# Two attentions on one core: A's maxima and sums in three halving steps, and additions moved from GpSimd to VectorE

## The chip, the cores and the metric

The kernel runs on one core of one Trainium2 chip. The metric is the device time of one execution in microseconds (us): the kernel before has a median of 1677.7 us over three runs (1677.5 to 1679.12).

The engines go by the profile's names: PE is TensorE (matmuls; PEld its weight loads), DVE is VectorE, ACT is ScalarE, POOL is GpSimd, and SP is SyncE, which issues nearly all DMA transfers. Each engine takes its instructions strictly in the order in which the program emits them, and an instruction that waits holds up all behind it on the same engine.

## The reference

Two attention layers over a sequence of 2048 positions, 576 features, 32 heads of 18 features, each with its own input, weights and output projection; their outputs stand side by side.

```python
# A: each position attends to itself and the 7 positions 2, 4, ... 14 before it
logits = jnp.einsum("bhsd,bhswd->bhsw", q, kg) * scale      # kg: 8 gathered keys per position
logits = jnp.where(mask[None, None, :, :], logits, -1e9)
attn = _softmax(logits, axis=-1)
o = jnp.einsum("bhsw,bhswd->bhsd", attn, vg)
# B: full attention, all 2048 keys
p = _softmax(jnp.einsum("bhqd,bhkd->bhqk", q, k) * scale, axis=-1)
o = jnp.einsum("bhqk,bhkd->bhqd", p, v)
# each: o (2048 x 576) @ wo
```

## The kernel before, in words

A first phase projects both inputs; the main loop (line 1099) is B's attention, and A's work is strewn into it.

**The main loop** has 512 steps: 8 groups of 4 heads, 4 blocks of 512 queries, 16 tiles of 128 keys. In one step TensorE makes four score tiles (`score`, L227, into four banks called "scores"), ScalarE takes their exponentials (L233), and TensorE weighs the values with those of the step before (`weigh`, L700, eight matmuls into `po`). Beside the scores TensorE forms three, in some steps four, score tiles of a later block (`take`, L162), of which VectorE keeps only the row maxima (`reduce`, L169). These go into a ring of three banks called "else": a fourth maximum's matmul must wait until VectorE has reduced the first.

**The order of the work** is written out by hand. `agenda` holds for each step a list of functions; `due` (L1114) calls them after that step's scores and weighing have been emitted, so what they emit stands on each engine between two steps' work. `plan(start, pieces)` enters functions at offsets from a start, `later(n, f)` at n steps from now. Nothing ties GpSimd's or SP's progress to the steps but the data: a step number gives only the place in the queue. `inside` holds functions that are called between the scores of the next step.

**A's attention** comes in 8 tiles j of 256 positions. `local(j)` makes the plan of a tile, which starts at step 10 + 54 j; offsets below are counted from there, so offset 59 of one tile is offset 5 of the next. The tile's 128 partitions hold 32 heads in 4 pieces of 64 positions. In order of the plan:

- `arrange(n)` (L802), n = 0, 1, 2 for q, k, v: a DRAM-to-DRAM transfer of A's projections into the tile's arrangement (`dpart<-da`, 576 or 702 KB), at offsets -24 to -22; `fetch` (L808) brings q (0), k (1) and v (28) from there into `aq` and `akv`.
- `match(c)` (L821), c = 0 to 8, at offset 5 + 5c // 2: on GpSimd a product of q and the 8 shifted keys for two features (L823) and, from c = 1 on, its addition (L827); the last one, at 25, also makes the 8 logits per position, `lg` (L830).
- `most` (29) and `lower` (30): VectorE reduces the maximum over the 8 into `am` (L837), GpSimd subtracts it (L844). `exponents` (32) on ScalarE. `total` (34): VectorE sums into `as` (L837) and takes its reciprocal (L851). `share` (35): GpSimd multiplies (L854).
- `weighted(c)` (L856), c = 0 to 8, at 36 + 5c // 2: four GpSimd instructions (L860 to L863) into the output `ao`.
- `upper` (58) and `rest` (59): GpSimd rounds the output into `aohi` (L867) and leaves the remainder in `ao` (L872). `put(0)`, `put(1)` (66, 67) store both to DRAM; `get` (74 and 81) brings them back transposed (`at`, `ahl`).
- `finished` leads to `sums_of_a` (L895) within the steps of offsets 79, 81, 86 and 88: the output projection for 128 positions and half the columns, with two maxima among its matmuls. `beside` (L965) returns two partial sums, `one` in a bank of "scores" and `two` in one of "else"; ScalarE copies `one` into `y` (L904), VectorE copies `two` into `part` (L905), GpSimd adds (L906).

GpSimd also serves B. After each 16 steps `finish` normalises a block's output with three instructions (L734 with `rec`, L735, L736) at 17 to 19 steps from the block's end; `halve` splits B's maxima (L107, L108). SP's queue carries, among others, the loads of B's rows for the next groups (`stack_loads`, L138 to L150, twelve transfers of 288 KB at steps 64 (g - 2) + 1 and on), `rec` (L733) and A's transfers.

Of the kernel before, what the change touches and what calls it, by code (L numbers as in the profile page):

```python
# [7 lines left out]
F32 = mybir.dt.float32  # L8
F32R = mybir.dt.float32r
BF16 = mybir.dt.bfloat16  # L10
AF = mybir.ActivationFunctionType
ALU = mybir.AluOpType
# [7 lines left out]
DH = 18  # L20
# [28 lines left out]
def ap(t, *dims):  # L49

    return bass.AP(tensor=t.tensor, offset=t.offset, ap=[list(t.ap[0])] + [list(d) for d in dims])
# [8 lines left out]
def two_attentions(ctx: ExitStack, tc, xa, wa, woa, xb, wb, wob, c_id, c_sel, out):  # L60
# [56 lines left out]
    def plan(start, pieces):  # L117
        for n, f in pieces:
            agenda[start + n].append(f)
# [100 lines left out]
    def score(g, b, kt, h, also, kind="scores"):  # L220

        assert (g, b) in placed
        qs, ks = sets[g % 3]
        p, r = divmod(h, 2)
        ps = bank(kind)
        at = slice(64 * r, 64 * r + 56)
        nc.tensor.matmul(ps, ks[at, p, 128 * kt : 128 * kt + 128], qs[at, b, p], start=True, stop=True)  # L227
        reduce = maximum(1 - r) if also else None

        counted[0] += 1  # L230
        early = counted[0] % 8 < 6
        e = (e_room if early else work).tile([128, 512], F32, name="e", bufs=6 if early else 2)
        nc.scalar.activation(e, ps, AF.Exp, scale=SCALE)  # L233
        if reduce:
            reduce()
        return e
# [560 lines left out]
    def local(j):  # L797

        st = {}
        p0 = AB * j  # L800

        def arrange(n):  # L802
            wide = (HALO if n else 0) + SUB
            load(rows(dparts[j][n][0, 0], (wide, D), (D * wide, 4), (1, wide)),
                 rows(da[D * n, HALO + p0 + SUB - wide :], (HALO + S, D), (SUB, 4), (1, wide)))


        def fetch(nm):  # L808
            halo = 0 if nm == "q" else HALO
            n = DH * (halo + SUB)  # L810
            t = st[nm] = work.tile([128, DH, halo + SUB], F32, name="akv" if halo else "aq", bufs=2 if halo else 1)
            load(ap(t, (1, n)), rows(dparts[j]["qkv".index(nm)][0, 0], (n, 128), (1, n)))

        def window(t, c):

            return ap(t[:, 2 * c, HALO:], (HALO + SUB, 2), (-DIL, W), (1, SUB))

        def wide():
            return work.tile([128, 2, W, SUB], F32, name="pr", bufs=2)

        def match(c):  # L821
            pr = wide()
            nc.gpsimd.tensor_mul(pr, ap(st["q"][:, 2 * c], (SUB, 2), (0, W), (1, SUB)), window(st["k"], c))  # L823
            if c == 0:
                st["pr"] = pr
            else:
                nc.gpsimd.tensor_add(st["pr"], st["pr"], pr)  # L827
            if c == DH // 2 - 1:
                lg = st["lg"] = work.tile([128, W, SUB], F32, name="lg", bufs=1)
                nc.gpsimd.tensor_add(lg, st["pr"][:, 0], st["pr"][:, 1])  # L830
                if j == 0:
                    for w in range(1, W):
                        nc.gpsimd.memset(lg[:32, w, : DIL * w], MASKED)

        def over_window(op, name):
            t = work.tile([128, SUB], F32, name=name, bufs=1)
            nc.vector.tensor_reduce(t, st["lg"].rearrange("p w i -> p i w"), axis=AX.X, op=op)  # L837
            return t

        def most():  # L840
            st["m"] = over_window(ALU.max, "am")

        def lower():
            nc.gpsimd.tensor_sub(st["lg"], st["lg"], ap(st["m"], (0, W), (1, SUB)))  # L844

        def exponents():
            nc.scalar.activation(st["lg"], st["lg"], AF.Exp, scale=SCALE)

        def total():
            s = st["s"] = over_window(ALU.add, "as")  # L850
            nc.vector.reciprocal(s, s)  # L851

        def share():
            nc.gpsimd.tensor_mul(st["lg"], st["lg"], ap(st["s"], (0, W), (1, SUB)))  # L854

        def weighted(c):  # L856
            if c == 0:
                st["o"] = work.tile([128, DH, SUB], F32, name="ao", bufs=1)
            at = wide()
            nc.gpsimd.tensor_mul(at, ap(st["lg"], (0, 2), (SUB, W), (1, SUB)), window(st["v"], c))  # L860
            nc.gpsimd.tensor_add(at[:, :, :4], at[:, :, :4], at[:, :, 4:])  # L861
            nc.gpsimd.tensor_add(at[:, :, :2], at[:, :, :2], at[:, :, 2:4])
            nc.gpsimd.tensor_add(st["o"][:, 2 * c : 2 * c + 2], at[:, :, 0], at[:, :, 1])  # L863

        def upper():
            hi = work.tile([128, DH, SUB], F32R, name="aohi", bufs=1)
            nc.gpsimd.tensor_copy(hi, st["o"])  # L867
            st["parts"] = hi, st["o"].bitcast(F32R)

        def rest():  # L870
            hi, lo = st["parts"]
            nc.gpsimd.tensor_sub(lo, st["o"], hi)  # L872

        def put(i):
            load(rows(dao[j, i, 0, 0], (DH * SUB, 128), (1, DH * SUB)),
                 ap(st["parts"][i].bitcast(F32), (1, DH * SUB)))

        def get(n):
            st["x"] = []
            st["n"] = n  # L880
            last = work.tile([128, 128], F32R, name="ahl", bufs=1)
            for i in range(2):
                t = work.tile([128, 4, 128], F32R, name=f"at{i}", bufs=1)
                for s in range(2):
                    load(t.bitcast(F32)[:, :, SUB * s : SUB * s + SUB],
                         dao[j, i, 2 * n + s, :512].rearrange("(c p) n -> p c n", p=128))
                load(last.bitcast(F32)[64 * i : 64 * i + 64].rearrange("p (s n) -> p s n", s=2),
                     rows(dao[j, i, 2 * n, 512], (SUB, 64), (D * SUB, 2), (1, SUB)))
                st["x"].append([t[:, c] for c in range(4)])
            st["x"].append(last)  # L890

        def finished(h):
            inside.append(lambda: sums_of_a(h))

        def sums_of_a(h):  # L895
            his, los = zip(*wo["a"])
            w = his[:4], los[:4], his[4], los[4]
            cols = slice(288 * h, 288 * h + 288)
            if h == 0:
                st["y"] = ys["a", j, st["n"]] = work.tile([128, D], F32, name="y", bufs=3)  # L900
            one, two = beside("scores", *(halves(r, 0, w, st["x"], cols, slice(0, 128), True) for r in range(2)))
            y = st["y"][:, cols]
            part = work.tile([128, 288], F32, name="part", bufs=2)
            nc.scalar.activation(y, one, AF.Copy)  # L904
            nc.vector.tensor_copy(part, two)  # L905
            nc.gpsimd.tensor_add(y, y, part)  # L906

        plan = {0: lambda: fetch("q"), 1: lambda: fetch("k"), 28: lambda: fetch("v"), 29: most, 30: lower,
                32: exponents, 34: total, 35: share, 58: upper, 59: rest, 66: lambda: put(0), 67: lambda: put(1)}
        for c in range(DH // 2):  # L910
            plan[5 + 5 * c // 2] = lambda c=c: match(c)
            plan[36 + 5 * c // 2] = lambda c=c: weighted(c)
        for n in range(3):
            plan[(-24 if j else -7) + n] = lambda n=n: arrange(n)
        for n in range(2):
            at = 74 + 7 * n
            plan[at] = lambda n=n: get(n)
            plan[at + 4] = lambda: finished(0)
            plan[at + 6] = lambda: finished(1)
            producing.update((A_FROM + GAP * j + at + 5, A_FROM + GAP * j + at + 7))  # L920
            plan[at + 12] = lambda n=n: load(out[p0 + 128 * n : p0 + 128 * n + 128, :D], ys["a", j, n])
        return plan


    olds = defaultdict(list)
# [33 lines left out]


    inside = []

    waiting = []

# [92 lines left out]
    ):  # L1057
        plan(start, [(4 * c, lambda k=k, src=src, ch=ch: load_wo(k, src, *ch)) for c, ch in enumerate(chunks)])
    for j in range(NJ):
        plan(A_FROM + GAP * j, local(j).items())  # L1060
    for g in range(1, NG):
        if g > EARLY:
            plan(STEPS * (g - 2) + 1, [(n, f) for n, f in enumerate(stack_loads(g))])
# [35 lines left out]
    while step < ALL:  # L1099
        n, kt = divmod(step, NT)  # L1100
        g, b = divmod(n, NB)
        places = positions(min(4 if behind() > 0 else 3, total - sum(given)))
        es = []
        for h in range(4):

            if inside and h == (3 if 3 in places else 2):
                inside.pop(0)()
            es.append(score(g, b, kt, h, h in places))
        while waiting:
            waiting.pop(0)()  # L1110
        if ready:
            weigh(*ready.pop(0))
        ready.append((g, b, kt, es))
        due()  # L1114
        if waiting:
            waiting.pop(0)()
        step += 1
# [30 lines left out]
```

## Time and profile before

| | |
|---|---|
| median of three runs | 1677.7 us |
| the profiled execution | 1677.95 us |
| its span, from the first to the last instruction | 1676.2 us |
| first weighing of the main loop | at 425.42 us |
| mean granted TensorE clock | 0.998 of full speed |
| PE, DVE, ACT, POOL busy in the span | 99%, 84%, 73%, 60% |
| between 500 and 700 us: DVE, ACT, POOL busy | 179.92, 186.30, 165.47 of 200 us |

A row of the timeline gives start, duration (us), engine, line, operation, what is written from what, shapes and count; equal instructions that follow each other are merged. In square brackets stands the idle time of the engine ahead of the row and what ended it. A row of groups gives count, then busy time and mean ns of one, then idle time. A row of the windows gives the stretch and its length, then the busy time of PE, PEld, DVE, ACT and POOL with their counts, the granted clock, the share of the DMA engines and GB/s.

### The profile page before, as it was taken

The numbers are of one execution on the slowest core, as the hardware profiler recorded it, in microseconds if no ns is written. First come the engines' busy times: TensorE is split into PE (matmuls) and PEld (weight loads), VectorE is DVE, ScalarE is ACT, GpSimd is POOL, SyncE is SP. The second block draws the span as 40 slices with busy tenths as digits, with TensorE's granted clock in tenths as the row PEclk, the third lists the DMA queues.
The fourth block names the chain that finished last, engine by engine and source line by source line (L and its number), as shares of the span: only waits on it lengthen the run. The fifth ranks groups of instructions, "written<-read, shape, count | busy, mean of one in ns | idle before, by whom it ended". The sixth has DMA issues, their size and how long they took to land.

```text
span 1676.2 us, 33705 instructions
## 1 busy us (share of the span) xinstructions
PE 1664.2 (99%) x12994; PEld 922.9 (55%) x12994; DVE 1410.6 (84%) x2318; ACT 1223.3 (73%) x2420; POOL 998.6 (60%) x842
## 2 busy tenths in 40 slices
PE   9999999999999999999999999999999999999998
PEld 7998888887433444344444344444444344344765
DVE  5199999999889989889889988889888989888433
ACT  6423521211999988988988987998988988988444
POOL 2306732100286996986984996986995997812010
PEclk9999999999999999999999999999999999999999
DMA  8938944421624536165247128227526222134101
GB/s 246 242 108 220 264 141 135 139 90 66 94 82 62 142 99 107 59 155 115 66 107 156 64 84 181 70 63 134 132 64 131 76 76 77 35 98 170 57 30 58
DMA packets 186082, 188.37 MB, mean 112 GB/s; under 512 B 114832, under 2 KB 129936, under 8 KB 184192
## 3 DMA queue, kind: packets, MB, share of 16 engines
q1 hardware_dynamic: 181056, 174.66, 40.1%
q0 software_dynamic: 4032, 10.63, 3.1%
q8 instruction: 102, 1.67, 0.4%
q10 hardware_dynamic: 832, 0.92, 0.2%
q14 instruction: 60, 0.49, 0.1%
HBM read 113.30 MB, written 88.12 MB: 120 GB/s over the span
## 4 chain that ended last, share of the span: by engine, by line
PE 89%; POOL 6%; SPq 2%; DVE 1%; DMA 1%; issue 1%; ACT 0%; POOLq 0%; ACTq 0%; DVEq 0%
PE po L700 27%; PE bank L227 21%; PE bank L320 14%; PE bank L162 14%; PE bank L979 7%; PE bank L257 4%; SPq L146 1%; POOL pr L823 1%; POOL pr L860 1%; POOL pr L827 1%; DVE mx L169 1%; POOL pr L861 1%; DMA rec<-drec 1%; PE bank L958 1%; PE bank L181 0%
## 5 line engine op out<-in xcount | busy, mean ns | idle before, releaser
L169 DVE TENSOR_REDUCE mx<-bank 128x1 f32<-128x512 f32 x2048 | 1294.4, 685 | 154.1 <-PE bank L162 132.0
L233 ACT ACTIVATE e<-bank 128x512 f32<-128x512 f32 x2048 | 1060.4, 610 | 108.6 <-PE bank L227 57.1
L162 PE MATMUL bank<-ks,qs 54*128 54x512 f32 x2048 | 757.6, 424 | 5.0 <-DVE mx L169 2.7
L227 PE MATMUL bank<-qs,ks 56*128 56x512 f32 x2048 | 582.9, 425 | 0.0
L227 PEld LDWEIGHTS bank<-qs,ks 56*128 56x128 f32 x2048 | 327.2, 186 | 430.7 <-ACT e L233 403.1
L700 PE MATMUL po<-e,v 128*19 128x512 f32 x4096 | 541.0, 600 | 0.0
L162 PEld LDWEIGHTS bank<-ks,qs 54*128 54x128 f32 x2048 | 342.8, 185 | 34.2 <-DVE mx L169 16.8
L823 POOL TENSOR_TENSOR pr<-aq,akv 128x1024 f32<-128x1024 f32 x72 | 157.9, 2197 | 24.6 <-PE po L700 22.3
L700 PEld LDWEIGHTS po<-e,v 128*19 128x19 f32 x4096 | 69.8, 97 | 181.7 <-issue 170.7
L860 POOL TENSOR_TENSOR pr<-lg,akv 128x1024 f32<-128x1024 f32 x72 | 158.1, 2195 | 0.3
L827 POOL TENSOR_TENSOR pr<-pr 128x1024 f32<-128x1024 f32 x64 | 152.4, 2382 | 5.0
L651 ACT ACTIVATE ohi<-bank 128x512 f32<-128x512 f32 (+1 forms) x56 | 30.4, 595 | 155.2 <-issue 124.4
L320 PE MATMUL bank<-xlo,ahi 64*128 64x512 f32 (+1 forms) x448 | 121.8, 391 | 0.1
L320 PE MATMUL bank<-xhi,alo 64*128 64x512 f32 (+1 forms) x448 | 118.6, 390 | 0.0
L320 PE MATMUL bank<-xhi,ahi 64*128 64x512 f32 (+1 forms) x448 | 115.2, 392 | 0.0
L906 POOL TENSOR_TENSOR y<-y,part 128x288 f32<-128x288 f32 x32 | 25.6, 799 | 117.8 <-DVE part L905 102.4
L861 POOL TENSOR_TENSOR pr<-pr 128x512 f32<-128x512 f32 x72 | 92.4, 1283 | 5.6
L461 POOL TENSOR_TENSOR olo<-olo,ohi 128x512 fp32r<-128x512 f32 x36 | 46.2, 1298 | 68.3 <-ACT ohi L460 67.1
L368 POOL TENSOR_TENSOR alo<-raw,ahi 128x512 fp32r<-128x512 f32 (+1 forms) x14 | 17.6, 1254 | 115.1 <-ACT ahi L367 90.6
L320 PEld LDWEIGHTS bank<-xlo,ahi 64*128 64x128 f32 (+1 forms) x448 | 68.1, 182 | 9.4 <-POOL xlo L368 0.5
L320 PEld LDWEIGHTS bank<-xhi,alo 64*128 64x128 f32 (+1 forms) x448 | 65.4, 182 | 9.1
L979 PE MATMUL bank<-wohi,at 64*128 64x288 f32 x512 | 68.9, 301 | 0.0
(194 smaller groups left out, 1845.4 us busy)
## 6 DMA issues: line engine op xcount, KB each, us to landing
do<-n SPq DMA_DIRECT2D x28, 512.0 KB
da<-ohi SPq DMA_DIRECT2D x52, 256.0 KB
dpart<-da SPq DMA_DIRECT2D x16, 702.0 KB
akv<-dpart SPq DMA_DIRECT2D x16, 702.0 KB
out<-y SPq DMA_DIRECT2D x32, 288.0 KB
qs<-dqk SPq DMA_DIRECT2D x30, 288.0 KB
ks<-dqk SPq DMA_DIRECT2D x30, 288.0 KB
at<-dao SPq DMA_DIRECT2D x64, 128.0 KB
```

Of the source, the lines that this page charges most:

```text
L162: nc.tensor.matmul(ps, qs[at, b, p, 128 * t : 128 * t + 128], ks[at, p, 512 * k : 512 * k + 512], start=True, stop=True)
L169: nc.vector.tensor_reduce(mx[:, r, p, t, k : k + 1], ps, axis=AX.X, op=ALU.max)
L227: nc.tensor.matmul(ps, ks[at, p, 128 * kt : 128 * kt + 128], qs[at, b, p], start=True, stop=True)
L233: nc.scalar.activation(e, ps, AF.Exp, scale=SCALE)
L257: nc.tensor.matmul(ps, a, b, start=c == i == 0, stop=c == 4 and i == 1)
L320: nc.tensor.matmul(ps, a, b, start=start, stop=stop)
L700: nc.tensor.matmul(po[32 * i : 32 * i + 19], vs[g][:, kt, 19 * i : 19 * i + 19], es[i], start=kt == 0, stop=kt == NT - 1)
L823: nc.gpsimd.tensor_mul(pr, ap(st["q"][:, 2 * c], (SUB, 2), (0, W), (1, SUB)), window(st["k"], c))
L827: nc.gpsimd.tensor_add(st["pr"], st["pr"], pr)
L860: nc.gpsimd.tensor_mul(at, ap(st["lg"], (0, 2), (SUB, W), (1, SUB)), window(st["v"], c))
L861: nc.gpsimd.tensor_add(at[:, :, :4], at[:, :, :4], at[:, :, 4:])
L979: nc.tensor.matmul(ps, a, b, start=start, stop=stop)
```

## The change

`most` and `total` no longer use one strided reduction over the 8: VectorE halves the 8 in three steps of 256, 128 and 64 elements a partition. The reciprocal becomes `inverse`, in two halves at two steps. `rest` goes from GpSimd to VectorE, in three parts at three steps. In `sums_of_a` ScalarE copies `two`, and VectorE adds `one` from its bank after all scores of the step (`outside`, emptied ahead of `waiting` and `weigh`). The offsets from `most` on move: `most` 29 to 32, `lower` 30 to 33, `exponents` 32 to 35, `total` 34 to 37, `share` 35 to 39, `weighted` from 36 on to 40 on, `upper` 58 to 62, `rest` 59 to 64, 65 and 66, `put` 66 and 67 to 67 and 68. `match` and `fetch` stay. `arrange` moves for two tiles: steps 202, 203, 204 become 206, 207, 208 for j = 4, and 256, 257, 258 become 270, 271, 272 for j = 5.

```diff
         def over_window(op, name):
-            t = work.tile([128, SUB], F32, name=name, bufs=1)
-            nc.vector.tensor_reduce(t, st["lg"].rearrange("p w i -> p i w"), axis=AX.X, op=op)
-            return t
+            t = st[name] = work.tile([128, W // 2, SUB], F32, name=name, bufs=1)
+            src = st["lg"]
+            for half in (W // 2, W // 4, 1):
+                nc.vector.tensor_tensor(t[:, :half], src[:, :half], src[:, half : 2 * half], op=op)
+                src = t
...
         def total():
-            s = st["s"] = over_window(ALU.add, "as")
-            nc.vector.reciprocal(s, s)
+            over_window(ALU.add, "as")
+
+        def inverse(n):
+            half = st["as"][:, 0, SUB // 2 * n : SUB // 2 * n + SUB // 2]
+            nc.vector.reciprocal(half, half)
...
-        def rest():
-            hi, lo = st["parts"]
-            nc.gpsimd.tensor_sub(lo, st["o"], hi)
+        def rest(i):
+            hi, lo, o = (t[:, DH // 3 * i : DH // 3 * (i + 1)] for t in (*st["parts"], st["o"]))
+            nc.vector.tensor_sub(lo, o, hi)
...
-            part = work.tile([128, 288], F32, name="part", bufs=2)
-            nc.scalar.activation(y, one, AF.Copy)
-            nc.vector.tensor_copy(part, two)
-            nc.gpsimd.tensor_add(y, y, part)
-
-        plan = {0: lambda: fetch("q"), 1: lambda: fetch("k"), 28: lambda: fetch("v"), 29: most, 30: lower,
-                32: exponents, 34: total, 35: share, 58: upper, 59: rest, 66: lambda: put(0), 67: lambda: put(1)}
+            nc.scalar.activation(y, two, AF.Copy)
+            outside.append(lambda: nc.vector.tensor_add(y, one, y))
+
+        plan = {0: lambda: fetch("q"), 1: lambda: fetch("k"), 28: lambda: fetch("v"), 32: most, 33: lower,
+                35: exponents, 37: total, 39: share, 62: upper, 67: lambda: put(0), 68: lambda: put(1)}
+
+        short = [(at + n, lambda f=f, n=n: f(n)) for f, at, many in ((inverse, 38, 2), (rest, 64, 3)) for n in range(many)]
         for c in range(DH // 2):
             plan[5 + 5 * c // 2] = lambda c=c: match(c)
-            plan[36 + 5 * c // 2] = lambda c=c: weighted(c)
+            plan[40 + 5 * c // 2] = lambda c=c: weighted(c)
+        at = A_FROM + GAP * j - 24
+        at = max(at, STEPS * (at // STEPS) + 14) - A_FROM - GAP * j
         for n in range(3):
-            plan[(-24 if j else -7) + n] = lambda n=n: arrange(n)
+            plan[at + n if j else n - 7] = lambda n=n: arrange(n)
...
+        while outside:
+            outside.pop(0)()
         while waiting:
             waiting.pop(0)()
```

More of the change, by code (lines that the diff above doesn't have):

```diff
@@ L835, in over_window @@
         def over_window(op, name):
-            t = work.tile([128, SUB], F32, name=name, bufs=1)
-            nc.vector.tensor_reduce(t, st["lg"].rearrange("p w i -> p i w"), axis=AX.X, op=op)
-            return t
+            t = st[name] = work.tile([128, W // 2, SUB], F32, name=name, bufs=1)
[3 more added lines that the diff above has]
+                src = t
         def most():
-            st["m"] = over_window(ALU.max, "am")
+            over_window(ALU.max, "am")
         def lower():
-            nc.gpsimd.tensor_sub(st["lg"], st["lg"], ap(st["m"], (0, W), (1, SUB)))
+            nc.gpsimd.tensor_sub(st["lg"], st["lg"], ap(st["am"], (0, W), (1, SUB)))
         def exponents():
@@ L849, in total @@
         def total():
-            s = st["s"] = over_window(ALU.add, "as")
-            nc.vector.reciprocal(s, s)
+            over_window(ALU.add, "as")
+        def inverse(n):
+            half = st["as"][:, 0, SUB // 2 * n : SUB // 2 * n + SUB // 2]
+            nc.vector.reciprocal(half, half)
         def share():
-            nc.gpsimd.tensor_mul(st["lg"], st["lg"], ap(st["s"], (0, W), (1, SUB)))
+            nc.gpsimd.tensor_mul(st["lg"], st["lg"], ap(st["as"], (0, W), (1, SUB)))
         def weighted(c):
@@ L921, in local @@
             plan[at + 12] = lambda n=n: load(out[p0 + 128 * n : p0 + 128 * n + 128, :D], ys["a", j, n])
-        return plan
+        return [*short, *plan.items()]
     olds = defaultdict(list)
@@ L961, in two_attentions @@
     inside = []
+    outside = []
     waiting = []
@@ L1059, in two_attentions @@
     for j in range(NJ):
-        plan(A_FROM + GAP * j, local(j).items())
+        plan(A_FROM + GAP * j, local(j))
     for g in range(1, NG):
```

## The prediction

> **What bounds the kernel now.** First the page: one engine is busy for the whole span.
>
> ```profile
> span 1676.2 us, 33705 instructions
> PE 1664.2 (99%) x12994; PEld 922.9 (55%) x12994; DVE 1410.6 (84%) x2318; ACT 1223.3 (73%) x2420; POOL 998.6 (60%) x842
> L169 DVE TENSOR_REDUCE mx<-bank 128x1 f32<-128x512 f32 x2048 | 1294.4, 685 | 154.1 <-PE bank L162 132.0
> ```
>
> So time is lost or won only where TensorE stalls, and the groups say who can stall it: VectorE, whose queue is full of B's maxima (L169). Then the timeline of two ordinary steps of the main loop (four scores, three maxima, one weighing, L700):
>
> ```profile
> 1004.93 1.89 DVE L169 TENSOR_REDUCE mx<-bank 128x1 f32<-128x512 f32 x3 [0.23 <-PE bank L162]
> 1005.49 1.05 PE L700 MATMUL po<-e,v 128*19 128x512 f32 x8
> 1007.62 1.05 PE L700 MATMUL po<-e,v 128*19 128x512 f32 x8
> ```
>
> A step is 2.13 us (1007.62 less 1005.49); VectorE needs 1.89 of it, so it catches up 0.24 us a step. Next the stretch in which tile j = 1 takes its maxima and sums:
>
> ```profile
> 628.27 1.05 PE L700 MATMUL po<-e,v 128*19 128x512 f32 x8
> 629.51 1.05 DVE L837 TENSOR_REDUCE am<-lg 128x64 f32<-128x512 f32 x1
> 630.39 1.05 PE L700 MATMUL po<-e,v 128*19 128x512 f32 x8
> 633.06 1.05 PE L700 MATMUL po<-e,v 128*19 128x512 f32 x8
> 637.35 1.05 PE L700 MATMUL po<-e,v 128*19 128x512 f32 x8
> 644.16 1.05 PE L700 MATMUL po<-e,v 128*19 128x512 f32 x8
> 645.12 1.07 DVE L837 TENSOR_REDUCE as<-lg 128x64 f32<-128x512 f32 x1
> 646.22 0.55 DVE L851 RECIPROCAL as<-as 128x64 f32<-128x64 f32 x1
> 646.29 1.05 PE L700 MATMUL po<-e,v 128*19 128x512 f32 x8
> 648.99 1.05 PE L700 MATMUL po<-e,v 128*19 128x512 f32 x8
> ```
>
> After `am` the next step takes 2.67 us (633.06 less 630.39), after `as` 2.70 (648.99 less 646.29): 0.54 and 0.57 over a plain step. A 1.05 us addition costs 0.54, so VectorE may run late by 0.5 us before TensorE stops (three banks for maxima). A step with sums of A is 4.29 (637.35 less 633.06). `am` starts 1.24 us after its step's weighing (629.51 less 628.27), `as`, behind a step with sums, 0.96 after (645.12 less 644.16). Last, what a long wait on VectorE costs, at j = 4:
>
> ```profile
> 1008.36 1.27 POOL L830 TENSOR_TENSOR lg<-pr 128x512 f32<-128x512 f32 x1
> 1009.66 1.03 DVE L837 TENSOR_REDUCE am<-lg 128x64 f32<-128x512 f32 x1 [2.84 <-POOL lg L830]
> 1011.35 0.79 PE L162 MATMUL bank<-ks,qs 54*128 54x512 f32 x1 [2.24 <-DVE mx L169]
> 1013.69 1.91 PE L700 MATMUL po<-e,v 128*19 128x512 f32 x8
> 1019.70 1.05 PE L700 MATMUL po<-e,v 128*19 128x512 f32 x8
> 1013.00:1015.00 2.00, 2.00 (x11) 0.20 (x9) 1.28 (x3) 1.39 (x3) 0.27 (x1) 0.50 1.37 94
> ```
>
> `am` came to the head of VectorE before GpSimd had `lg`; nothing behind it could run. From 1007.62 to 1019.70 is 12.08 us for a plain step and one with sums, 5.66 over 2.13 + 4.29. VectorE was taken for 2.84 + 1.03 = 3.87, less the 0.5: 3.4 us of stall. The other 2.3 is the clock: 0.50 is granted in the last row (sixth figure from its start), matmuls take 0.79 and weighing 1.91. The Trainium skill, "TensorE: Matmul & The Clock Gate", Part 1, has the clock halved after idling and restored after some 3.4 us of activity, an estimate of 1.7 us lost each time; this trace shows 2.3.
>
> **The change, part by part.** *Maxima and sums.* Two-input operations on VectorE, with 512 and with 288 elements, and the reciprocals:
>
> ```profile
> 25.87 0.69 DVE L404 TENSOR_TENSOR xhl<-raw,ohi 64x512 fp32r<-64x512 f32 x1
> L999 DVE TENSOR_TENSOR y<-bank,y 128x288 f32<-128x288 f32 x24 | 11.0, 458 | 2.5
> L731 DVE RECIPROCAL den<-den 128x16 f32<-128x16 f32 x29 | 7.0, 243 | 0.0
> L905 DVE COPY part<-bank 128x288 f32<-128x288 f32 x32 | 14.3, 448 | 0.0
> L906 POOL TENSOR_TENSOR y<-y,part 128x288 f32<-128x288 f32 x32 | 25.6, 799 | 117.8 <-DVE part L905 102.4
> ```
>
> On the line through 0.69 and 0.458 the steps of 256, 128 and 64 elements take 0.42, 0.29 and 0.23: 0.94 us as an estimate, hardly less than the 1.05. But `most` moves from offset 29 to 32, behind a step with sums, where VectorE is 0.28 earlier: stall 0.94 - 0.28 - 0.5 = 0.16 in place of 0.54, 0.38 saved in each of seven tiles (2.7), and at j = 4, where `lg` has three steps more, 5.66 - 0.16 = 5.5. `total` stalls 0.94 - 0.5 = 0.44, and the half reciprocals (0.35 each, between 0.243 and 0.55) 0.35 - 0.24 = 0.11 twice: 0.66 for 0.57, 0.7 lost in eight tiles. Sum: **7.5 us won**.
>
> *Output sums.* VectorE gives up a copy of 0.448 and takes an add of 0.458 x32: nothing, as steps with sums leave it time. GpSimd loses 32 x 0.8 = 26 us, but at offsets 25 to 34 where it waits anyway (102.4). A score bank is now freed by the add, behind the step's last maximum; its next user is the third score of the next step:
>
> ```profile
> 644.52 0.68 DVE L169 TENSOR_REDUCE mx<-bank 128x1 f32<-128x512 f32 x1
> 645.73 0.63 PE L227 MATMUL bank<-qs,ks 56*128 56x512 f32 x2
> ```
>
> 644.52 + 0.68 + 0.46 = 645.66, in time for 645.73: nothing; 0.2 x 32 = 6 us if the add comes 0.3 later.
>
> *Arranges, and SP's queue.* At j = 3 a late `rec`, held behind B's loads and the arranges, stopped GpSimd.
>
> ```profile
> 905.21 0.59 SPq L733 DMA_DIRECT2D rec<-drec x1
> 914.08 1.29 POOL L734 TENSOR_TENSOR o<-o,rec 128x512 f32<-128x512 f32 x1 [9.64 <-DMA rec<-drec]
> ```
>
> Without that wait `lg` of j = 4 is earlier; the gain is the 5.5 already counted. The moved arranges stand 10 steps or more ahead of their fetches, so those wait for nothing. `put(0)` and `put(1)` wait on SP for `upper` and `rest`; behind them stand B's small loads and, at 74, `get`: with `upper` near 67 they go out a step late at most, for sums at 79: nothing.
>
> *Low parts.* Here I see the large term. `rest`, three subtractions of 384 elements (0.56 each on the same line), now stands in VectorE's queue at offsets 64 to 66, and the first waits for `upper` on GpSimd. Behind each are queued three maxima, for whose banks TensorE waits. Is `upper` done by then? GpSimd at j = 1 before:
>
> ```profile
> 646.86 1.28 POOL L854 TENSOR_TENSOR lg<-lg,as 128x512 f32<-128x512 f32 x1 [0.75 <-DVE as L851]
> 648.09 1.28 POOL L736 TENSOR_TENSOR n<-o,n 128x512 fp32r<-128x512 f32 x1
> 655.34 1.05 PE L700 MATMUL po<-e,v 128*19 128x512 f32 x8
> 697.11 1.14 POOL L867 CAST aohi<-ao 128x1152 fp32r<-128x1152 f32 x1
> 708.81 1.05 PE L700 MATMUL po<-e,v 128*19 128x512 f32 x8
> L823 POOL TENSOR_TENSOR pr<-aq,akv 128x1024 f32<-128x1024 f32 x72 | 157.9, 2197 | 24.6 <-PE po L700 22.3
> L827 POOL TENSOR_TENSOR pr<-pr 128x1024 f32<-128x1024 f32 x64 | 152.4, 2382 | 5.0
> ```
>
> From `share` (646.86) to the end of `upper` (698.25) GpSimd works 51.4 us without a pause. In the changed program's order on GpSimd, `upper` (offset 62) also stands behind the next tile's first `match` (59) and second (61): two products of 2.20 and an add of 2.38, with 0.08 between each 7.0 us. One L736 (1.25 with its turn) falls out of the stretch at j = 1: 51.4 + 7.0 - 1.25 = 57.2. j = 4 and 6 have the same list, j = 3 one L736 more (58.4), j = 0, 2 and 5 one normalisation more (L734, L735, L736: 3.3; 60.5). From the weighing of offset 39 (655.34) to that of 64 (708.81) are 53.5 us. `share` starts some 0.8 later within its step than VectorE reaches `rest` in its own (0.4 late after `total`, 0.35 reciprocal, a little hand-over). So VectorE waits 57.2 + 0.8 - 53.5 = 4.5 us at j = 1, 4, 6; 5.7 at j = 3; 7.8 at j = 0, 2, 5; at j = 7 no `match` follows and it waits for nothing. Together 13.5 + 5.7 + 23.4 = **42.6 us**, in each of the seven tiles past the point at which the clock fell: each adds 0.56 - 0.5 + 2.3 = 2.4, together 16.5.
>
> Then the two engines disturb each other. The trace's first such meeting:
>
> ```profile
> 19.98 1.29 POOL L461 TENSOR_TENSOR olo<-olo,ohi 128x512 fp32r<-128x512 f32 x1 [19.04 <-ACT ohi L460]
> 20.45 1.37 DVE L368 TENSOR_TENSOR xlo<-raw,xhi 128x512 fp32r<-128x512 f32 x1 [0.98 <-ACT xhi L367]
> ```
>
> The subtraction took 1.37 us instead of 0.69: GpSimd ended at 21.27, and it ended 0.55 later. As `upper` ends, GpSimd goes on to `match` (2.20) and VectorE to `rest(0)`: it loses nothing if it is first, 2.2 if not; no row decides, I take 1.1, seven times: 7.7 (0 to 15.4). `rest(1)` and `rest(2)` meet GpSimd too, in steps at half clock where VectorE has room: nothing, up to 2 us a tile if the clock is back. The Trainium skill, "SBUF — State Buffer", Who interferes with whom, says the same: with two SBUF inputs VectorE contends with a GpSimd instruction that reads SBUF, and the second blocks until the first is done. The trace agrees (1.37 for 0.69).
>
> **Sum.** 42.6 + 16.5 + 7.7 - 7.5 = 59.3 us more. The profiled execution took 1677.95 (span 1676.2 and 1.75 around it), 0.25 over the median shown: 1677.95 + 59.3 = **1737 us**.
>
> **Rivals.**
> 1. `upper` is in time (GpSimd runs 8 us shorter than I add up), but each `rest` meets GpSimd: 3 x (0.56 + 1.1) - 0.5 - 2 x 0.24 = 4.0 a tile, 28 in seven, 0.7 at j = 7; less 7.5: +21, 1699 us. For it: the row of 1.37. Against: the order on GpSimd.
> 2. Faster: `upper` is in time and VectorE gets its operands at once, 3 x 0.56 - 0.98 = 0.7 a tile, 5.6 in eight, less 7.5, less the odd longer `as` stalls (some 2): -4, 1674 us. The point from which it decides: `upper` ends before VectorE reaches offset 64, which needs the two `match` steps (7.0 us) out of the way. For it: without them the wait at j = 1 would be negative (4.5 - 7.0).
> 3. `rest` gets no operand while GpSimd runs without a pause, some 30 us of `match`: 7 x 25 on top, about 1900 us. Against: the subtraction above did get in.
>
> **How the numbers follow.** Forecast 0.75, rival 1 0.10, rival 2 0.11, rival 3 0.04. Within the forecast: waits 7 us either way, clock 1.7 to 3.2 each (4 less, 6 more), the meeting 0 to 15.4, later meetings up to 14. This gives 1718 to 1768; the range reaches to rival 1: 1688 to 1770. Chances: faster by over 0.2% 0.09, within 0.2% (about what a measurement of this kernel can tell) 0.03, slower 0.88.
>
> **What would show it.** Right: VectorE's first subtraction into `ao` has an idle time of 4 to 8 us before it, released by `aohi` on GpSimd, in seven of eight tiles, and the clock falls to 0.50 seven times; GpSimd's row of y adds is gone; the wait of 2.84 before `am` at j = 4 too. Wrong: `aohi` ends before the subtraction is reached, or the clock stays at 1.00.

## The result, and the profile after

The changed kernel takes 1732.27 us (median of five runs, 1730.66 to 1733.47) against 1677.63 us for the kernel before: a ratio of 1.0326, 95% interval 1.0315 to 1.0337, so 3.3% slower. The forecast was 1737 us. Its profiled execution took 1731.63 us, with a span of 1729.8. One slow execution of a later kernel, of 5314.29 us with `rest` back on GpSimd, counts in no ratio below.

The first rows of its page, and the group of the maxima:

```profile
span 1729.8 us, 33722 instructions
PE 1681.7 (97%) x12994; PEld 930.9 (54%) x12994; DVE 1437.0 (83%) x2382; ACT 1224.2 (71%) x2420; POOL 957.2 (55%) x802
L169 DVE TENSOR_REDUCE mx<-bank 128x1 f32<-128x512 f32 x2048 | 1294.6, 684 | 146.6 <-PE bank L162 121.2
```

The same matmuls are there, but TensorE is 97% busy instead of 99%, and busy for 17.5 us longer, at a mean granted clock of 0.981 for 0.998. GpSimd lost 41 us of work. Most of the lost time stands around one group, the subtractions that moved to VectorE:

```profile
L878 DVE TENSOR_TENSOR ao<-ao,aohi 128x384 fp32r<-128x384 f32 x24 | 29.1, 1211 | 33.9 <-POOL aohi L873 33.9
```

VectorE stood idle 33.9 us in front of them until GpSimd had finished `aohi`, and they took 1211 ns on average, where one takes 0.55 us at j = 7, when GpSimd has little left to do. The timeline of tile j = 2 shows the chain:

```profile
851.71 1.05 PE L700 MATMUL po<-e,v 128*19 128x512 f32 x8
853.02 2.34 POOL L827 TENSOR_TENSOR pr<-pr 128x1024 f32<-128x1024 f32 x1
855.31 1.26 POOL L736 TENSOR_TENSOR n<-o,n 128x512 fp32r<-128x512 f32 x1
856.52 1.14 POOL L873 CAST aohi<-ao 128x1152 fp32r<-128x1152 f32 x1
857.62 2.17 POOL L823 TENSOR_TENSOR pr<-aq,akv 128x1024 f32<-128x1024 f32 x1
857.70 2.51 DVE L878 TENSOR_TENSOR ao<-ao,aohi 128x384 fp32r<-128x384 f32 x1 [6.78 <-POOL aohi L873]
860.86 0.79 PE L162 MATMUL bank<-ks,qs 54*128 54x512 f32 x1 [7.66 <-DVE mx L169]
863.03 1.91 PE L700 MATMUL po<-e,v 128*19 128x512 f32 x8
866.12 1.05 PE L700 MATMUL po<-e,v 128*19 128x512 f32 x8
```

GpSimd is still at the next tile's `match` (L827) and at a normalisation when VectorE is already waiting. When `aohi` is done (857.66), both engines may go on, and GpSimd's next product seems to be served first: the subtraction ends at 860.21, 0.42 us after that product (859.79). TensorE was idle for 7.66 us, and two steps took 14.41 us (866.12 less 851.71) instead of 4.25: 10.2 us lost. The windows over this stretch show the clock in the sixth figure behind the length:

```profile
853.00:855.00 2.00, 0.20 (x1) 0.00 (x0) 0.00 (x0) 0.79 (x2) 1.98 (x1) 0.97 0.00 0
855.00:859.00 4.00, 0.00 (x0) 0.00 (x0) 1.30 (x1) 0.00 (x0) 4.00 (x4) 0.50 0.00 0
859.00:863.00 4.00, 2.14 (x6) 1.32 (x6) 4.00 (x7) 0.88 (x2) 3.84 (x3) 0.50 0.00 0
863.00:867.00 4.00, 4.00 (x24) 1.07 (x23) 3.76 (x8) 2.29 (x6) 3.92 (x2) 0.74 0.70 263
```

It is at half speed from some 1.7 us after TensorE stopped (853.20) until some 4 us after it went on (860.86). All tiles, from the same kinds of rows (us); the last column adds up the two or three weighing-to-weighing steps that are longer than plain ones:

| j | wait forecast | wait | first subtraction | steps over plain ones |
|---|---|---|---|---|
| 0 | 7.8 | 7.18 | 2.51 | 10.9 |
| 1 | 4.5 | 4.07 | 0.61 | 7.0 |
| 2 | 7.8 | 6.78 | 2.51 | 10.2 |
| 3 | 5.7 | 1.05 | 2.54 | 5.2 |
| 4 | 4.5 | 3.62 | 1.61 | 7.4 |
| 5 | 7.8 | 7.13 | 2.51 | 10.3 |
| 6 | 4.5 | 4.13 | 2.51 | 7.8 |
| 7 | none | none | 0.55 | 0.2 |

The seven come to 58.8 us. Maxima and sums, which were to win 7.5 us, at j = 1:

```profile
642.37 1.05 PE L700 MATMUL po<-e,v 128*19 128x512 f32 x8
646.65 1.05 PE L700 MATMUL po<-e,v 128*19 128x512 f32 x8
648.79 1.05 PE L700 MATMUL po<-e,v 128*19 128x512 f32 x8
661.83 1.05 PE L700 MATMUL po<-e,v 128*19 128x512 f32 x8
664.28 1.05 PE L700 MATMUL po<-e,v 128*19 128x512 f32 x8
666.40 1.05 PE L700 MATMUL po<-e,v 128*19 128x512 f32 x8
```

Behind `am` the step is plain (648.79 less 646.65 = 2.14, where it was 2.67). Behind `as` it is 2.45 (664.28 less 661.83), 0.33 over a plain one. The first half reciprocal costs nothing (2.12); the second falls into a step that takes 2.42, from 666.40 to 668.82, where the same step of the kernel before took 2.31 (657.46 to 659.77): 0.44 in all for what was 0.57. The long stall at j = 4 (5.66 us) is gone: the two steps take 6.48 us where they took 12.08. But a new one stands at j = 3, which I had not foreseen:

```profile
913.85 15.60 SPq L804 DMA_DIRECT2D dpart<-da  x3
929.55 6.44 SPq L730 DMA_DIRECT2D den<-o  x1
942.60 1.05 PE L700 MATMUL po<-e,v 128*19 128x512 f32 x8
944.63 0.25 DVE L731 RECIPROCAL den<-den 128x16 f32<-128x16 f32 x1 [2.83 <-DMA den<-o]
945.49 0.50 PE L162 MATMUL bank<-ks,qs 54*128 54x512 f32 x1 [1.40 <-DVE mx L169]
947.54 1.91 PE L700 MATMUL po<-e,v 128*19 128x512 f32 x8
950.99 1.05 PE L700 MATMUL po<-e,v 128*19 128x512 f32 x8
```

The moved arranges hold SP's queue for 15.60 us and the small load of `den` behind them for 6.44; VectorE waits 2.83 us for it, TensorE stops for 1.40, and the clock falls again (weighing 1.91): 950.99 less 942.60 is 8.39 us for two steps, 4.1 too many. Together 58.8 + 4.1, and the spans differ by 53.6, so the rest of the change wins 9.3 us.

### The profile page after: what moved, and what is told of

The parts are those of the page before. It is cut to its first block, busy times and chain, and to the rows that moved or that the text cites. A ratio compares the mean times of both kernels' runs of the same rounds, so it can differ in the third digit from the quotient of the medians.

```text
span 1729.8 us, 33722 instructions
## 1 busy us (share of the span) xinstructions
PE 1681.7 (97%) x12994; PEld 930.9 (54%) x12994; DVE 1437.0 (83%) x2382; ACT 1224.2 (71%) x2420; POOL 957.2 (55%) x802
## 4 chain that ended last, share of the span: by engine, by line
PE 72%; POOL 20%; DVE 4%; issue 2%; DMA 1%; ACT 0%; SPq 0%; POOLq 0%; DVEq 0%
PE po L700 19%; PE bank L227 15%; PE bank L320 14%; PE bank L162 11%; POOL pr L866 7%; PE bank L990 7%; PE bank L257 4%; POOL pr L867 4%; DVE mx L169 3%; POOL pr L868 2%; POOL pr L823 2%; POOL ao L869 1%; DVE ao L878 1%; POOL n L736 1%; POOL pr L827 1%
## 5 line engine op out<-in xcount | busy, mean ns | idle before, releaser
L700 PE MATMUL po<-e,v 128*19 128x512 f32 x4096 | 548.5, 607 | 0.0
L162 PEld LDWEIGHTS bank<-ks,qs 54*128 54x128 f32 x2048 | 347.9, 187 | 70.1 <-DVE mx L169 53.1
L827 POOL TENSOR_TENSOR pr<-pr 128x1024 f32<-128x1024 f32 x64 | 154.4, 2412 | 5.0
L107 POOL CAST mh<-mt 16x128 fp32r<-16x128 f32 x32 | 9.7, 303 | 119.3 <-DVE mt L183 119.3
L847 POOL TENSOR_TENSOR lg<-lg,am 128x512 f32<-128x512 f32 x8 | 10.2, 1278 | 114.5 <-DVE am L840 94.7
```

The lines of the kernel that those rows point to most:

```text
L162: nc.tensor.matmul(ps, qs[at, b, p, 128 * t : 128 * t + 128], ks[at, p, 512 * k : 512 * k + 512], start=True, stop=True)
L700: nc.tensor.matmul(po[32 * i : 32 * i + 19], vs[g][:, kt, 19 * i : 19 * i + 19], es[i], start=kt == 0, stop=kt == NT - 1)
```

## The experiments

My theory: the loss is `rest` on VectorE, and in it the wait for `upper` with the clock's fall is the larger part, the meeting with GpSimd the smaller. Rivals: the meeting alone; other parts of the change (banks freed later, arranges); GpSimd late for another reason than the two `match`. Each ratio stands against executions of the kernel before that were measured beside it. Their medians are 1677.07 us for the experiments on the place of `rest` and on one reduction, 1674.23 for those on `match`, on the arranges and on the output sums with one buffer, and 1677.3 for the last two. So medians of different groups can't be compared to better than some 3 us.

**`rest` back on GpSimd** (the change without that part):

```diff
-            nc.vector.tensor_sub(lo, o, hi)      # rest(i), offsets 64 to 66
+            nc.gpsimd.tensor_sub(lo, st["o"], hi)      # rest, whole, offset 63
```

> The changed kernel, with rest alone put back on GpSimd, whole, at offset 63 right behind upper. Theory (VectorE's first subtraction waits for upper, TensorE stops, its clock halves, and the subtraction meets GpSimd's instructions): the 58.8 us that the steps around the subtractions take over plain ones go, 1732.3 - 58.8 = about 1674 us, and no stretch at half clock at offset 64. Unless lg of the next tile becomes late for the maxima, since GpSimd gets 2.66 us a tile back: then some tiles wait in front of am instead. Rival (the loss lies in the other parts, the score bank that is freed later or the moved arranges): it stays above 1710 us.

1674.98 us, ratio 0.9984 (0.9972 to 0.9996). The page of this kernel:

```profile
span 1675.2 us, 33706 instructions
PE 1664.0 (99%) x12994; PEld 924.3 (55%) x12994; DVE 1413.5 (84%) x2358; ACT 1223.0 (73%) x2420; POOL 974.5 (58%) x810
```

TensorE's busy time is that of before. The whole loss is `rest`; the other parts together win a little, though VectorE still waits for `den` twice (3.6 us).

**`rest` alone, on the kernel before** (with the three-part `rest(i)` of the change):

```diff
-                ... 58: upper, 59: rest, 66: lambda: put(0), 67: lambda: put(1)}
+                ... 58: upper, 67: lambda: put(0), 68: lambda: put(1)}
+        plan.update({64 + n: lambda n=n: rest(n) for n in range(3)})      # rest(i) on VectorE
```

> The kernel before, with one part of the change alone: rest in three parts on VectorE at offsets 64 to 66, put at 67 and 68; upper stays at 58, ahead of the next tile's match. Theory: upper is done in time (it ended near offset 59 in seven tiles), so no wait for it; what remains is the meeting with GpSimd, 0.55 us and up to 2 us more for each of 21 subtractions beyond the 0.5 us that TensorE bears: 1690 to 1708 us. Rival 1 (the meeting alone makes the loss, the wait is small): near 1730 us. Rival 2 (VectorE gets its operands at once): 1683 us at most.

1690.11 us, ratio 1.0085 (1.0070 to 1.0100): the lower edge of what I expected. Its group, and the one tile whose `upper` was late:

```profile
L872 DVE TENSOR_TENSOR ao<-ao,aohi 128x384 fp32r<-128x384 f32 x24 | 30.8, 1282 | 0.8 <-POOL aohi L867 0.8
```

```profile
969.21 4.29 POOL L823 TENSOR_TENSOR pr<-aq,akv 128x1024 f32<-128x1024 f32 x2
969.28 4.65 DVE L872 TENSOR_TENSOR ao<-ao,aohi 128x384 fp32r<-128x384 f32 x1 [0.79 <-POOL aohi L867]
```

The waits are gone (0.8 us in all), the meetings are all there (1282 ns on average), and the kernel loses 13 us, not 55. The 13 are a net figure: in the trace the steps around the subtractions take 20.3 us more than in the kernel before, and 5.1 come back at j = 4, where `lg` is now done 4.7 us before `am` starts (1015.70 and 1020.43). Once a subtraction lost to two of GpSimd's instructions in a row (4.65 us).

**`rest` five steps later**, in the changed kernel:

```diff
-        ... (rest, 64, 3) ...      67: lambda: put(0), 68: lambda: put(1)
+        ... (rest, 69, 3) ...      69: lambda: put(0), 72: lambda: put(1)
```

> The changed kernel, with rest at offsets 69 to 71 instead of 64 to 66, put(0) at 69 and put(1) at 72. upper ends at most 7.2 us (some 3.4 steps) after VectorE reached offset 64, so five steps later it is done. Theory: the waits (33.9 us) and the half clock go, the meetings stay: 1680 to 1700 us. Rival 1 (the meeting alone): above 1720 us.

1685.84 us, ratio 1.0054 (1.0039 to 1.0070). The group:

```profile
L878 DVE TENSOR_TENSOR ao<-ao,aohi 128x384 fp32r<-128x384 f32 x24 | 22.6, 940 | 0.0
```

No wait: some 46 us of the 54.6 lost come back by the place in the queue alone. The meetings remain, but are shorter too (940 ns on average for 1211), so not all of the 46 is the wait and its clock. The clock did not keep its full speed either, as I had expected it to: it fell once with the wait for `den`, and once at j = 1, where the first subtraction took 2.58 us without any wait for `aohi`:

```profile
724.27 0.50 PE L162 MATMUL bank<-ks,qs 54*128 54x512 f32 x1 [0.86 <-DVE mx L169]
726.61 1.91 PE L700 MATMUL po<-e,v 128*19 128x512 f32 x8
```

**The two `match` behind `upper`**, in the changed kernel with `rest` at 64:

```diff
-            plan[5 + 5 * c // 2] = lambda c=c: match(c)
+            plan[5 + 5 * c // 2 if c > 1 else 8 + c] = lambda c=c: match(c)
```

> The changed kernel, with the next tile's first two match at offsets 8 and 9 (behind upper, at 62) instead of 5 and 7. Theory (these two stand ahead of upper on GpSimd and make it 7.0 us late): the waits of 4 to 7 us in front of the first subtraction shrink by 7.0 us to none or nearly none, the meetings stay, and so does the wait for den: 1680 to 1695 us. Rival (upper is late for another reason): above 1710 us.

1696.11 us, ratio 1.0129 (1.0116 to 1.0142), 1 us above the band I gave (21.9 above the kernel before beside it) and below the rival's 1710. Its group:

```profile
L878 DVE TENSOR_TENSOR ao<-ao,aohi 128x384 fp32r<-128x384 f32 x24 | 32.1, 1336 | 1.3 <-POOL aohi L873 1.3
```

Waits of 1.3 us in place of 33.9: it was these two functions in GpSimd's queue that made `upper` late. The meetings stay, at 1336 ns the longest of all, and at j = 0, 2 and 3 the clock still fell to 0.50 after them.

**One reduction** for the maxima and one for the sums, with the reciprocal whole behind the sum, at the later offsets, on the first experiment:

```diff
-            for half in (W // 2, W // 4, 1):
-                nc.vector.tensor_tensor(t[:, :half], src[:, :half], src[:, half : 2 * half], op=op)
-                src = t
+            nc.vector.tensor_reduce(t[:, 0], st["lg"].rearrange("p w i -> p i w"), axis=AX.X, op=op)
...
```

> As the first kernel (rest on GpSimd), but maxima and sums at the later offsets each in one strided reduction and the reciprocal whole behind the sum, as before. Theory (the gain is the later start behind a step with sums and in time for lg, not the three steps): 1 to 4 us slower than the first kernel, from the sums alone (1.05 + 0.55 at once for 0.94, 0.34 and 0.34). Rival (the three short steps make the gain): 8 us or more slower than the first kernel.

1675.49 us, ratio 0.9992 (0.9983 to 1.0002), against 0.9984 (0.9972 to 0.9996) with three steps: not to be told apart. The maxima win as much with one reduction as with three steps, so it is not the steps that win there; the later start is what remains. But the equal times hide two effects that the traces show. The step behind the sums takes 3.04 us at j = 1 (from 651.37) where it takes 2.47 in the first experiment (from 651.11), and it is 0.56 to 0.60 longer in seven of the eight tiles; and at j = 7 the step behind the maxima takes 4.47 (from 1393.46) where the three steps made it 7.68 (from 1393.52).

**Arranges as before**, on the first experiment (`at = -24` for all tiles):

> As the first kernel (rest on GpSimd), and arrange for all tiles at offset -24 as before. In the first kernel VectorE waits for the load of den at steps 216 and 280 (2.04 and 1.55 us), held on SP behind the moved arranges, and the steps there take some 4.6 us over plain ones. Theory (the moved arranges cost this, and maxima that start later no longer need lg early): those waits go, 2 to 5 us faster than the first kernel. Rival (the move is a gain, since rec is late again without it and with it lg): as slow as the first kernel or slower, with a wait of VectorE for lg in front of am at j = 4.

1673.04 us, ratio 0.9995 (0.9985 to 1.0006). That is 1.9 us below the first experiment by the medians and no gain by the ratios, so the 2 to 5 us that I expected are not shown. The waits for `den` are gone from its trace, and GpSimd waits longer for `rec` (30.3 us in two waits, against 14.8 in one) without delaying `am`: at j = 4 the step behind `am` is plain (2.11). So the stall at j = 4 goes without the moved arranges.

**Arranges ahead of B's loads** (`at = {4: 179, 5: 243}.get(j, at) - A_FROM - GAP * j`), on the first experiment:

> As the first kernel, with the two moved arranges ahead of B's loads instead of behind them: j = 4 at steps 179 to 181, j = 5 at 243 to 245. Theory: neither den nor rec is held up, 3 to 6 us faster than the first kernel and the fastest of all: about 1670 us. Rival (any place of the transfers holds something up): no faster than the first kernel.

1672.34 us, ratio 0.9987 (0.9978 to 0.9996). `den` comes in time and GpSimd waits for `rec` once, 3.2 us; but the 3 to 6 us that I expected are not shown: 2.6 by the medians, none by the ratios. One step stands out, at j = 7, with 6.42 us (1388.12 to 1394.54):

```profile
1387.09 0.91 DVE L840 TENSOR_TENSOR am<-lg 128x256 f32<-128x256 f32 x1
1388.04 2.06 DVE L840 TENSOR_TENSOR am<-am 128x128 f32<-128x128 f32 x2
1388.61 1.41 POOL L108 TENSOR_TENSOR ks<-y,qs 126x576 fp32r<-126x576 f32 x1
1390.75 0.49 PE L162 MATMUL bank<-ks,qs 54*128 54x512 f32 x1 [1.14 <-DVE mx L169]
```

The maxima's steps have two SBUF inputs as well, and here they meet GpSimd splitting B's output weights: 0.91 and 2.06 us, where j = 1 of the changed kernel took 0.41 and 0.55.

**Output sums as before**, on the experiment before this:

```diff
-            nc.scalar.activation(y, two, AF.Copy)
-            outside.append(lambda: nc.vector.tensor_add(y, one, y))
+            part = work.tile([128, 288], F32, name="part", bufs=1)
+            nc.scalar.activation(y, one, AF.Copy)
+            nc.vector.tensor_copy(part, two)
+            nc.gpsimd.tensor_add(y, y, part)
```

> As the kernel with the arranges ahead, with A's output sums as before: ScalarE copies one, VectorE copies two (part, one buffer), GpSimd adds. Theory (the add on VectorE costs nothing, the 26 us on GpSimd stood where it waits): within 2 us of it. Rival (the score bank that is freed later costs TensorE time): 3 us or more faster.

1687.43 us, ratio 1.0073 (1.0058 to 1.0089), against both expectations. The cause was in my variant: one buffer for `part` where there had been two.

```profile
L911 DVE COPY part<-bank 128x288 f32<-128x288 f32 x32 | 14.4, 450 | 12.8 <-POOL y L912 12.6
```

VectorE waited 12.6 us for GpSimd's adds. So with two buffers, `am` and `as` sharing a tile to make room:

> As the kernel with the arranges ahead, with A's output sums as before and two buffers for part, as before (am and as share one tile to make room). With one buffer VectorE waited up to 4.0 us in front of part for GpSimd's add of the half before. Theory (one buffer made the loss; the add on VectorE itself costs and wins nothing): those waits are gone, within 2 us of the kernel with the arranges ahead, about 1672 us. Rival (GpSimd has no time for the 26 us of adds, so something of A is late): above 1680 us.

```profile
L911 DVE COPY part<-bank 128x288 f32<-128x288 f32 x32 | 14.3, 448 | 0.1
```

1671.40 us, ratio 0.9964 (0.9952 to 0.9976), and no wait of note. The median is 0.9 us below that of the kernel with the arranges ahead, and the spans of the two traces are 1669.1 and 1668.1 us: so far as they tell, the move of the sums to VectorE neither costs nor wins. By the ratios it would cost some 4 us (0.9987 against 0.9964), but these stand against different medians of the kernel before, so this stays open. What the move surely saves is the buffer.

**The maxima in one reduction, the sums in three steps**, on the kernel with the arranges ahead:

> As the kernel with the arranges ahead, with the maxima in one strided reduction and the sums in three steps. There the three maxima steps of j = 7 met GpSimd's instructions (0.91 and 2.06 us for two, for 0.42 and 0.52) and the step took 2.1 us more. Theory (a reduction has one input and does not meet GpSimd): that stall goes, the step with 6.42 us falls to 4.4, 2 us faster than the kernel with the arranges ahead. Rival (the longer reduction stalls TensorE by 0.3 us in each tile): as fast as it.

1669.71 us (1668.77 to 1670.5), ratio 0.9954 (0.9942 to 0.9966): some 0.5% faster than the kernel before, and so faster than the changed one too. At j = 7:

```profile
1387.18 1.05 PE L700 MATMUL po<-e,v 128*19 128x512 f32 x8
1388.26 1.09 DVE L840 TENSOR_REDUCE am<-lg 128x64 f32<-128x512 f32 x1
1389.30 1.05 PE L700 MATMUL po<-e,v 128*19 128x512 f32 x8
```

The reduction takes its 1.09 us, its step 2.12 and the next, which had taken 6.42, now 4.48 (1389.30 to 1393.78). The Trainium skill, "SBUF — State Buffer", Who interferes with whom, says that `tensor_reduce` never contends with GpSimd on this chip; the trace agrees: 1.05 in the kernel before with GpSimd waiting, 1.09 here with GpSimd at work (L736 and a cast). These 1.9 us of one step are what the two traces show for this part; the 2.6 us between the medians are from different groups.

## Why the prediction was right

- *The wait for `upper`*: right in cause, and near in size. 42.6 us forecast, 33.9 measured, shorter by 0.4 to 1.0 in six tiles. At j = 3 it is 1.05 for 5.7: TensorE had lost 4.1 us to `den` some 45 us earlier while GpSimd worked on, which would account for most of it. My sign asked for 4 to 8 us in seven tiles; five are in it, j = 4 is at 3.62 and j = 3 at 1.05. That the two `match` make the wait is shown by putting them behind `upper`.
- *The clock*: it fell in all seven tiles, as forecast (16.5 us, in which the subtraction's own time over the slack is 0.4). Its share was not tried apart; by difference 58.8 - 33.9 - 10.9 = 14.0 us are left for it and for the later subtractions. The meetings alone can make it fall too: with the two `match` behind `upper` it did at three tiles, with waits of 0.5 us or less.
- *The meeting*: 7.7 us forecast at half of 2.2 a tile. The first subtractions took 10.9 us over seven times 0.55: five of them took 2.5 us, one 1.61 and one 0.61. The mean was a poor guess between two ends; the sum stayed within my 0 to 15.4.
- *Together* the steps around `rest` cost 58.8 us where I added up 66.8 (42.6 + 16.5 + 7.7).
- *Maxima and sums*: 7.5 us forecast, 9.3 by difference. The stall behind `am` fell to nothing (0.16 forecast), that behind `as` to 0.44 (0.66), and the stall at j = 4 went; it went without the moved arranges too. That three steps bring the maxima next to nothing, as 0.94 for 1.05 says, the one-reduction kernel shows. For the sums, the three steps with the reciprocal halved save some 0.58 us a tile against one reduction and a whole reciprocal at the same offset.
- *Output sums*: nothing forecast, and nothing seen in the traces with two buffers; the ratios leave up to 4 us open.
- *Arranges*: here a step failed. "The moved arranges stand 10 steps or more ahead of their fetches, so those wait for nothing": true of the fetches, but I did not ask what stands behind the arranges on SP. It was `den`, and it cost 4.1 us at j = 3.
- *The total*: that it came within 5 us is in part luck. The waits were 8.7 us too long in my sum, the clock with the later subtractions 2.5, and the maxima and sums won 1.8 more; the first meetings cost 3.2 more, and `den`, which I had at nothing, 4.1. The upper end of my 1718 to 1768 is also wrong: 7, 6, 7.7 and 14 on top of 1737 make 1772, above the 1770 of the range.
- *Rival 1* (meetings alone, 1699 us) comes near to what the kernel with the two `match` behind `upper` made true, at 1696; *rival 2* needed no meeting and was not seen, nor was *rival 3*.

## What to carry to other kernels

Before an instruction moves to an in-order engine that feeds the bottleneck, add up what stands ahead of its input on the other engine, everything in that queue, not only the step number at which it was planned. A guard of two steps is worth nothing when two other functions of 7 us have slipped into the queue. And work taken from an engine that waits anyway wins only where its lateness reached the bottleneck, here at most at j = 4, while each instruction on a nearly full engine is paid as soon as it exceeds the slack, here 0.5 us.

## What the runs showed of the hardware that I had not expected

- When `aohi` was done and VectorE's subtraction and GpSimd's next instruction could both start, the subtraction took 2.51 to 2.54 us for 0.55 in five tiles of seven, and once, in the kernel with `rest` alone, 4.65, past two of GpSimd's instructions. So in these traces a waiting subtraction did not always get in when GpSimd passed from one instruction to the next.
- TensorE's clock fell after an idle time of only 1.40 us (weighing 1.91 instead of 1.05 in the stall for `den`), and with `rest` five steps later after 0.86. But the length of the idle time alone does not decide: with the two `match` behind `upper`, at j = 5, weighing kept its 1.05 us after 1.44.

```profile
1233.97 0.50 PE L162 MATMUL bank<-ks,qs 54*128 54x512 f32 x1 [1.44 <-DVE mx L169]
1235.58 1.05 PE L700 MATMUL po<-e,v 128*19 128x512 f32 x8
```
